# Second products of experts 2 to 4 in four forms: one bank, two banks by turns, columns in runs of 128 or of 32

## The chip, the core and the metric

The kernel runs on one core of a Trainium2 chip. The metric is the device time of one execution in microseconds, the median of the timed runs.

## The reference

Attention with band masks (2 batches, 8 heads, 576 positions, width 64) gives 1152 tokens of width 512. They go through a mixture of four experts, weighted by normalised domain probabilities, and then through one wider gated layer:

```python
def _moe_ref(x, domain_probs, w1, w2):
    p = domain_probs / (domain_probs.sum(-1, keepdims=True) + 1e-09)
    for e in range(E):
        h = np.maximum(x @ w1[e], 0.0)
        out += p[:, e:e + 1] * (h @ w2[e])
def _moe2_ref(x, w_in, w_out):
    h = x @ w_in
    g = h * (1.0 / (1.0 + np.exp(-1.702 * h)))
    return g @ w_out
```

The hidden width is 1024 in an expert and 2048 in the last layer. The weights of the last layer come as 64-bit floats.

## The kernel before

Every matrix is split into a high part of the type that TensorE multiplies in one pass (float32r, 4 bytes) and the low remainder, so each product of the algorithm is three matmuls: high by high, high by low, low by high.

The first expert is computed beside the attention (lines 517 and 545 to 547). From the second expert on the work goes in steps `s`. A step is 256 of the hidden columns: steps 4 to 15 are experts 2 to 4 (four steps each), steps 16 to 23 the last layer. Each step is done for two blocks of tokens, `c` = 0 with 512 tokens (four tiles of 128) and `c` = 1 with 640 (five tiles).

- `first2(s, c, slots)` makes the hidden values. Seven block products by a Strassen-like scheme, each six matmuls of 256 (`c` = 0) or 320 (`c` = 1) columns, are written to four tiles of the PSUM pool `ps`, named ga to gd in the trace (line 781). ACT, DVE and POOL combine them (lines 796 to 839) into `h`, high and low. The last of these steps is put on a list, `deferred`.
- `second2(s, c, slots)` (lines 849 to 879) multiplies `h` with the second weights. For each tile of tokens it takes one whole PSUM bank (128x512 floats) of the pool `pacc`, which has three, by turns: `pa0`, `pa1`, `pa2`. Six matmuls of 512 columns add up in it (lines 863 to 865, for two halves `o`). Then DVE multiplies by the expert's probability and adds to `acc` in SBUF (line 868, the eviction). After each tile one entry of `deferred` and one share of the queued side work (`slots`) are issued.

The side work is the preparation of coming weights: splitting (ACT line 685 and others, POOL lines 667 to 686), and the conversion of the 64-bit weights (ACT 727 and 728, DVE 733 and 737, POOL 738, stores and loads by SP). `due` says which lists are handed out during which call.

The order of the calls is written out by `order_of`: the first products of one block ahead of the second products of the block before. In the middle of experts 2 to 4 it reads: first products of (5, 1), second of (5, 0), first of (6, 0), second of (5, 1), and so on. Each engine executes its instructions in that order and waits on semaphores.

Of the kernel before, what the change touches and what calls it, by code (L numbers as in the profile page):

```python
# [8 lines left out]
F32 = mybir.dt.float32  # L9
# [3 lines left out]
AF = mybir.ActivationFunctionType  # L13
ALU = mybir.AluOpType
AX = mybir.AxisListType

P = 128
# [6 lines left out]
def fused_kernel(ctx: ExitStack, tc: tile.TileContext, q, k, v, dp, w1, w2, w_in, w_out, out):  # L24
# [17 lines left out]
    nc = tc.nc  # L42
    B, H, S, D = q.shape
    NT, DM = out.shape
    E, _, FF1 = w1.shape
# [17 lines left out]
    pacc = ctx.enter_context(tc.tile_pool(name="pacc", bufs=1, space=bass.MemoryType.PSUM))  # L63
# [8 lines left out]
    pw = const.tile([P, NC * NTI, E], F32, name="pw")  # L72
# [6 lines left out]
    acc = accp.tile([P, NC * NTI, DM], F32, name="acc")  # L79
# [417 lines left out]
    pa = {}  # L497
# [66 lines left out]
    SM, SE = NF * E, NF * E + F2 // 2  # L564
    TILES = (range(0, 4), range(4, 9))
    queue = []
    turn_ = [0]
# [6 lines left out]
    def slot(left):  # L574

        for _ in range(-(-len(queue) // max(left, 1))):
            queue.pop(0)()
# [186 lines left out]
    deferred = []  # L764
# [80 lines left out]
    def slots():  # L845
        slot(left[0])
        left[0] -= 1

    def second2(s, c, slots):
        n = N_[c]  # L850
        e, fp = divmod(s, NF)
        moe = e < E
        h = hbuf2.pop((s, c))
        wh, wl = wt[s, 1]
        for i, t in enumerate(TILES[c]):

            end = s == SE - 1 and c == 1 and i == len(TILES[c]) - 1
            for cols in (slice(0, DM // 2), slice(DM // 2, DM)) if end else (slice(0, DM),):
                pt = pacc.tile([P, 512], F32, tag=f"pa{turn_[0] % 3}", name=f"q{s}_{t}_{cols.start}")[:, cols]
                turn_[0] += 1  # L860
                for o in range(2):
                    hi, lo = (h[:, y, o * 2 * n + i * P:o * 2 * n + (i + 1) * P] for y in range(2))
                    nc.tensor.matmul(pt, hi, wh[:, o, cols], start=o == 0, stop=False)  # L863
                    nc.tensor.matmul(pt, hi, wl[:, o, cols], start=False, stop=False)  # L864
                    nc.tensor.matmul(pt, lo, wh[:, o, cols], start=False, stop=o == 1)  # L865
                dst = acc[:, t, cols]
                if moe:
                    nc.vector.scalar_tensor_tensor(dst, pt, pw[:, t, e:e + 1], dst, op0=ALU.mult, op1=ALU.add)  # L868
                elif s == SM and c == 1:
                    nc.vector.tensor_scalar_mul(dst, pt, 0.5)  # L870
                elif s == SM:
                    nc.scalar.activation(dst, pt, AF.Copy, scale=0.5)
                else:
                    nc.vector.scalar_tensor_tensor(dst, pt, 0.5, dst, op0=ALU.mult, op1=ALU.add)  # L874
                if s == SE - 1:
                    nc.sync.dma_start(out=out[t * P:(t + 1) * P, cols], in_=dst)
            if deferred:
                deferred.pop(0)()
            slots()

    seq = [("e", 0, c, f) for c in range(NC) for f in range(F1)]
    it_now = [0]
# [127 lines left out]
    for kind, (s, c) in pe:  # L1010
        todo = due(kind, s, c)
        if todo:
            assert not queue
            left[0] = todo[0]
            bg(*todo[1])
        (first2 if kind == "1" else second2)(s, c, slots)
# [29 lines left out]
```

## Time and profile before

| | |
|---|---|
| two timed runs | 649.69 and 650.69 us, median 650.19 |
| profiled execution, span from first to last instruction | 647.3 us |
| its own time beside the span | not recorded apart; the median is 2.9 us above the span |
| PE busy | 637.3 us, 98% |
| DVE, ACT, POOL busy | 419.6, 288.9, 356.2 us |
| matmuls | 4065, of which 362 stand on each of lines 863 to 865 |

PE is TensorE's matmuls, PEld its weight loads, which run beside them. Times of instructions are microseconds from the start of the span, unless marked ns. The duration of a matmul overlaps with that of the next, so what a product costs is read from start to start. [...]

### The profile page before, as it was taken

The numbers are of one execution on the slowest core, as the hardware profiler recorded it, in microseconds if no ns is written. First come the engines' busy times: TensorE is split into PE (matmuls) and PEld (weight loads), VectorE is DVE, ScalarE is ACT, GpSimd is POOL, SyncE is SP. The second block draws the span as 40 slices with busy tenths as digits, with TensorE's granted clock in tenths as the row PEclk, the third lists the DMA queues.
The fourth block names the chain that finished last, engine by engine and source line by source line (L and its number), as shares of the span: only waits on it lengthen the run. The fifth ranks groups of instructions, "written<-read, shape, count | busy, mean of one in ns | idle before, by whom it ended". The sixth has DMA issues, their size and how long they took to land.

```text
span 647.3 us, 10999 instructions
## 1 busy us (share of the span) xinstructions
PE 637.3 (98%) x4065; PEld 564.1 (87%) x4065; DVE 419.6 (65%) x882; ACT 288.9 (45%) x669; POOL 356.2 (55%) x362
## 2 busy tenths in 40 slices
PE   9999999999999999999999999999899999999998
PEld 6788888898898998998988988988798898898896
DVE  5775553296667667667667667557856767667655
ACT  6774342134444453443543544445745443444321
POOL 5433220367577587587578568586467744553300
PEclk9999999999999999999999999999999999999999
DMA  8966300004255345454445453211002111100003
GB/s 209 233 170 155 126 1 2 1 1 146 65 164 163 100 162 162 110 161 157 132 147 150 143 155 134 98 67 32 34 2 65 66 34 52 46 2 1 2 0 147
DMA packets 50149, 61.41 MB, mean 95 GB/s; under 512 B 20464, under 2 KB 32688, under 8 KB 50096
## 3 DMA queue, kind: packets, MB, share of 16 engines
q1 hardware_dynamic: 50096, 60.72, 31.1%
q8 instruction: 32, 0.52, 0.3%
q14 instruction: 21, 0.17, 0.1%
HBM read 49.96 MB, written 10.75 MB: 94 GB/s over the span
## 4 chain that ended last, share of the span: by engine, by line
PE 90%; DVE 4%; ACT 3%; issue 1%; POOL 1%; DVEq 0%; ACTq 0%
PE q L863 12%; PE q L865 12%; PE q L864 12%; PE gd L781 9%; PE ga L781 9%; PE gc L781 9%; PE g L517 8%; PE gb L781 4%; PE pa L545 3%; PE pa L547 3%; PE pa L546 3%; DVE cc L825 1%; PE spin L418 1%; DVE h L829 1%; ACT th L822 1%
## 5 line engine op out<-in xcount | busy, mean ns | idle before, releaser
L863 PE MATMUL q<-w2h,h 128*128 128x512 f32 (+1 forms) x362 | 143.4, 396 | 1.3 <-ACT xf L648 1.1
L865 PE MATMUL q<-w2h,h 128*128 128x512 f32 (+1 forms) x362 | 142.9, 395 | 0.0
L864 PE MATMUL q<-w2l,h 128*128 128x512 f32 (+1 forms) x362 | 142.9, 395 | 0.0
L868 DVE SCALAR_TENSOR_TENSOR acc<-q,pw,acc 128x512 f32<-128x512 f32 x108 | 80.5, 748 | 36.7 <-PE q L865 35.2
L738 POOL TENSOR_TENSOR m<-m,sd 128x512 int32<-128x512 int32 x32 | 41.9, 1308 | 78.3 <-issue 46.6
L863 PEld LDWEIGHTS q<-w2h,h 128*128 128x128 f32 x362 | 68.2, 188 | 17.2 <-ACT xf L648 1.5
L865 PEld LDWEIGHTS q<-w2h,h 128*128 128x128 f32 x362 | 68.1, 188 | 16.3
L864 PEld LDWEIGHTS q<-w2l,h 128*128 128x128 f32 x362 | 68.2, 188 | 14.7
L805 POOL TENSOR_TENSOR cc<-s,u 128x256 f32<-128x256 f32 (+1 forms) x40 | 37.4, 935 | 58.5 <-DVE s L803 56.2
L675 POOL TENSOR_TENSOR wsl<-ss,wsh 128x512 fp32r<-128x512 f32 x40 | 53.8, 1366 | 19.8 <-ACT wsh L674 19.8
L686 POOL TENSOR_TENSOR w2l<-st,w2h 128x512 fp32r<-128x512 f32 x40 | 51.9, 1301 | 5.0 <-ACT w2h L685 5.0
L874 DVE SCALAR_TENSOR_TENSOR acc<-q,acc 128x512 f32<-128x512 f32 (+1 forms) x64 | 42.7, 678 | 15.0 <-PE q L865 13.9
L671 POOL TENSOR_TENSOR wal<-st,wah 128x512 fp32r<-128x512 f32 (+1 forms) x40 | 50.2, 1271 | 2.5 <-ACT wah L670 2.5
L796 ACT ACTIVATE s<-ga 128x256 f32<-128x256 f32 (+1 forms) x40 | 16.4, 409 | 77.7 <-PE ga L781 77.7
L781 PE MATMUL ga<-xh,wah 128*128 128x256 f32 (+1 forms) x160 | 47.5, 297 | 0.0
L781 PE MATMUL ga<-xl,wah 128*128 128x256 f32 (+1 forms) x160 | 47.3, 296 | 0.0
L781 PE MATMUL ga<-xh,wal 128*128 128x256 f32 (+1 forms) x160 | 47.2, 295 | 0.0
L685 ACT ACTIVATE w2h<-st 128x512 fp32r<-128x512 f32 x40 | 25.0, 627 | 48.2 <-PE q L864 48.2
L801 DVE TENSOR_TENSOR u<-gb,s 128x256 f32<-128x256 f32 (+1 forms) x40 | 18.2, 456 | 39.4 <-PE gb L781 36.8
L781 PE MATMUL gd<-t,wah 128*128 128x256 f32 (+1 forms) x160 | 33.5, 298 | 1.7 <-DVE s L803 1.7
L815 ACT ACTIVATE h<-cc 128x768 fp32r<-128x768 f32 (+1 forms) x24 | 22.3, 928 | 27.6 <-POOL cc L805 23.9
L826 ACT ACTIVATE h<-cc 128x256 fp32r<-128x256 f32 (+3 forms) x32 | 22.0, 686 | 27.1 <-DVE cc L825 27.0
(458 smaller groups left out, 1632.0 us busy)
## 6 DMA issues: line engine op xcount, KB each, us to landing
st<-in_moe_w_dram SPq DMA_DIRECT2D x32, 512.0 KB, 5.4
sd<-in_moe_w_in_dram SPq DMA_DIRECT2D x16, 512.0 KB, 4.2
sd<-in_moe_w_out_dram SPq DMA_DIRECT2D x16, 512.0 KB, 4.1
w<-m SPq DMA_DIRECT2D x32, 256.0 KB, 4.4
st<-w SPq DMA_DIRECT2D x16, 512.0 KB, 3.3
out_dram<-acc SPq DMA_DIRECT2D x8, 256.0 KB, 2.0
v10big<-in_v_dram SPq DMA_DIRECT2D x2, 144.0 KB, 4.4
v11big<-in_v_dram SPq DMA_DIRECT2D x2, 144.0 KB, 2.8
```

The source lines that it names most:

```text
L517: nc.tensor.matmul(pt[:, :C], w[:, kt, fs], xx[:, kt, c * C:(c + 1) * C], start=first and y == 0, stop=not todo and y == len(products[x]) - 1)
L671: fns.append(lambda dst=dst, srcs=srcs: nc.gpsimd.tensor_tensor(out=al[:, dst], in0=srcs, in1=ah[:, dst].bitcast(F32), op=ALU.subtract))
L675: fns.append(lambda dst=dst: nc.gpsimd.tensor_tensor(out=sl[:, dst], in0=sums[:, dst], in1=sh[:, dst].bitcast(F32), op=ALU.subtract))
L686: fns.append(lambda o=o: nc.gpsimd.tensor_tensor(out=lo[:, o], in0=t[:, o], in1=hi[:, o].bitcast(F32), op=ALU.subtract))
L738: nc.gpsimd.tensor_tensor(out=m.bitcast(I32), in0=m.bitcast(I32), in1=t.bitcast(I32)[:, :, 0], op=ALU.add)
L781: nc.tensor.matmul(bank_[:, :n], wz[:, y, m, :], xz, start=start and m == 0 and z == 0, stop=m == 1 and z == 2, skip_group_check=not start)
L805: nc.gpsimd.tensor_tensor(out=cc[:, 3], in0=s75, in1=u2, op=ALU.add)
L863: nc.tensor.matmul(pt, hi, wh[:, o, cols], start=o == 0, stop=False)
L864: nc.tensor.matmul(pt, hi, wl[:, o, cols], start=False, stop=False)
L865: nc.tensor.matmul(pt, lo, wh[:, o, cols], start=False, stop=o == 1)
L868: nc.vector.scalar_tensor_tensor(dst, pt, pw[:, t, e:e + 1], dst, op0=ALU.mult, op1=ALU.add)
L874: nc.vector.scalar_tensor_tensor(dst, pt, 0.5, dst, op0=ALU.mult, op1=ALU.add)
```

## The change

In experts 2 to 4 the step number modulo 4 picks a form for the second products. Form 0 is as before. Form 1 takes the tiles in pairs: two banks are taken, and each of the six matmuls is issued for the one tile and then for the other; both evictions and two shares of side work follow the pair (a fifth tile stands alone). Forms 2 and 3 are as before, but a matmul reads its 512 weight columns and writes its bank in another order: the columns are cut into runs of 128 (form 2) or 32 (form 3), and all even runs come before all odd ones, on both sides alike.

```diff
-        for i, t in enumerate(TILES[c]):
+        form = s % 4 if moe else 0
+        tiles = list(enumerate(TILES[c]))
+        size = 2 if form == 1 else 1
+        for some in (tiles[x:x + size] for x in range(0, len(tiles), size)):
...
-                pt = pacc.tile([P, 512], F32, tag=f"pa{turn_[0] % 3}", name=f"q{s}_{t}_{cols.start}")[:, cols]
-                turn_[0] += 1
+                banks = []
+                for i, t in some:
+                    banks.append(pacc.tile([P, 512], F32, tag=f"pa{turn_[0] % 3}", name=f"q{s}_{t}_{cols.start}")[:, cols])
+                    turn_[0] += 1
                 for o in range(2):
-                    hi, lo = (h[:, y, o * 2 * n + i * P:o * 2 * n + (i + 1) * P] for y in range(2))
-                    nc.tensor.matmul(pt, hi, wh[:, o, cols], start=o == 0, stop=False)
-                    nc.tensor.matmul(pt, hi, wl[:, o, cols], start=False, stop=False)
-                    nc.tensor.matmul(pt, lo, wh[:, o, cols], start=False, stop=o == 1)
+                    for y in range(3):
+                        for (i, t), pt in zip(some, banks):
+                            hi, lo = (h[:, z, o * 2 * n + i * P:o * 2 * n + (i + 1) * P] for z in range(2))
+                            left_, right_ = ((hi, wh), (hi, wl), (lo, wh))[y]
+                            to, by = pt, right_[:, o, cols]
+                            if form >= 2:
+                                to, by = (z.rearrange("p (b a w) -> p a b w", a=2, w=128 if form == 2 else 32)
+                                          for z in (to, by))
+                            nc.tensor.matmul(to, left_, by, start=o == 0 and y == 0, stop=o == 1 and y == 2)
...
+            for _ in some:
+                if deferred:
+                    deferred.pop(0)()
+                slots()
```

On PE, in step 5 at the third and fourth tile of `c` = 0, before. A row is line, operation, bank's tile (q5_3 is step 5, tile 3) <- weights (w2h high, w2l low) and h, shape, and the semaphores waited for:

```order
L864 MATMUL q5_1_0_2530<-w2l_5_2188,h5_0_2369 128x512
L865 MATMUL q5_1_0_2530<-w2h_5_2187,h5_0_2369 128x512
L863 MATMUL q5_2_0_2540<-w2h_5_2187,h5_0_2369 128x512
L864 MATMUL q5_2_0_2540<-w2l_5_2188,h5_0_2369 128x512
L865 MATMUL q5_2_0_2540<-w2h_5_2187,h5_0_2369 128x512
L863 MATMUL q5_2_0_2540<-w2h_5_2187,h5_0_2369 128x512
L864 MATMUL q5_2_0_2540<-w2l_5_2188,h5_0_2369 128x512
L865 MATMUL q5_2_0_2540<-w2h_5_2187,h5_0_2369 128x512
L863 MATMUL q5_3_0_2549<-w2h_5_2187,h5_0_2369 128x512 [waits DVE_49]
```

The same place after:

```order
L875 MATMUL q5_0_0_2519<-w2l_5_2188,h5_0_2369 128x512 [waits Pool_49]
L875 MATMUL q5_1_0_2520<-w2l_5_2188,h5_0_2369 128x512
L875 MATMUL q5_0_0_2519<-w2h_5_2187,h5_0_2369 128x512
L875 MATMUL q5_1_0_2520<-w2h_5_2187,h5_0_2369 128x512
L875 MATMUL q5_2_0_2540<-w2h_5_2187,h5_0_2369 128x512
L875 MATMUL q5_3_0_2541<-w2h_5_2187,h5_0_2369 128x512 [waits DVE_49]
L875 MATMUL q5_2_0_2540<-w2l_5_2188,h5_0_2369 128x512
L875 MATMUL q5_3_0_2541<-w2l_5_2188,h5_0_2369 128x512
```

The wait of tile 3 for the eviction of tile 0, which had the same bank, stood twelve products behind tile 0's last product; now two products of other tiles stand between, the last one of tile 1 and the first one of tile 2.

On DVE at the same place, before (acc is an eviction, h the low part of the hidden values, m the word conversion):

```order
L839 TENSOR_TENSOR cc5_1_2449<-gd5_1_2444,u2_5_1_2447 128x320 [waits PE_49]
L868 SCALAR_TENSOR_TENSOR acc_92<-q5_0_0_2519,pw_87,acc_92 128x512 [waits PE_49]
L818 SCALAR_TENSOR_TENSOR h5_1_2498<-cc5_1_2449,h5_1_2498 128x960 [waits Activation_49]
L733 TENSOR_SCALAR m4_2528<-sd4_2327 128x512 [waits DMAHW5_49,DMAHW0_49]
L868 SCALAR_TENSOR_TENSOR acc_92<-q5_1_0_2530,pw_87,acc_92 128x512 [waits PE_49]
L737 SCALAR_TENSOR_TENSOR m4_2528<-sd4_2327,m4_2528 128x512 [waits DVE_49]
L868 SCALAR_TENSOR_TENSOR acc_92<-q5_2_0_2540,pw_87,acc_92 128x512 [waits PE_49]
```

And after:

```order
L839 TENSOR_TENSOR cc5_1_2449<-gd5_1_2444,u2_5_1_2447 128x320 [waits PE_49]
L879 SCALAR_TENSOR_TENSOR acc_92<-q5_0_0_2519,pw_87,acc_92 128x512 [waits PE_49]
L879 SCALAR_TENSOR_TENSOR acc_92<-q5_1_0_2520,pw_87,acc_92 128x512 [waits PE_49]
L818 SCALAR_TENSOR_TENSOR h5_1_2498<-cc5_1_2449,h5_1_2498 128x960 [waits Activation_49]
L733 TENSOR_SCALAR m4_2536<-sd4_2327 128x512 [waits DMAHW5_49,DMAHW0_49]
L737 SCALAR_TENSOR_TENSOR m4_2536<-sd4_2327,m4_2536 128x512 [waits DVE_49]
L879 SCALAR_TENSOR_TENSOR acc_92<-q5_2_0_2540,pw_87,acc_92 128x512 [waits PE_49]
```

The second eviction moved ahead of the low part of h and of the word conversion.

In step 7 (form 3) the first tile's six products read as follows after the change; the shape names the columns as 2 by 8 by 32, and the first product has a wait of PE for its own semaphore, which before it had not:

```order
L875 MATMUL q7_0_0_3023<-w2h_7_2691,h7_0_2873 128x2x8x32 [waits PE_49]
L875 MATMUL q7_0_0_3023<-w2l_7_2692,h7_0_2873 128x2x8x32 [waits Pool_49]
L875 MATMUL q7_0_0_3023<-w2h_7_2691,h7_0_2873 128x2x8x32 x2
L875 MATMUL q7_0_0_3023<-w2l_7_2692,h7_0_2873 128x2x8x32 [waits Pool_49]
L875 MATMUL q7_0_0_3023<-w2h_7_2691,h7_0_2873 128x2x8x32
```

The order of these products is as before. The awaited product is one of tile 6 of step 6, which had the same bank and is issued 55 products earlier.

## Rows read from the trace of the kernel before

**Rows 1.** The page: span, busy time of three engines, chain that ended last.

```profile
span 647.3 us, 10999 instructions
...
PE 637.3 (98%) x4065; PEld 564.1 (87%) x4065; DVE 419.6 (65%) x882; ACT 288.9 (45%) x669; POOL 356.2 (55%) x362
...
PE 90%; DVE 4%; ACT 3%; issue 1%; POOL 1%; DVEq 0%; ACTq 0%
```

**Rows 2.** Idle time of PE by releaser: us in total, times, longest us.

```profile
PE gd L781 <- DVE s L803: 1.7, 3, 0.9
...
PE q L863 <- ACT xf L648: 1.1, 1, 1.1
...
PE gc L781 <- POOL wsl L675: 0.2, 1, 0.2
```

**Rows 3.** Stretches: length, busy PE, PEld, DVE, ACT, POOL; granted clock, DMA share, GB/s.

```profile
177.00:201.00 24.00, 24.00 (x142) 21.54 (x141) 16.12 (x28) 10.56 (x20) 16.68 (x16) 1.00 0.49 143
391.00:415.00 24.00, 24.00 (x141) 21.54 (x140) 16.33 (x29) 10.72 (x20) 16.77 (x16) 1.00 0.33 121
```

**Rows 4.** PE in time, step 5: start us, us, instruction; 320-, 512-, 256-column products.

```profile
188.69 0.31 PE L781 MATMUL ga<-xh,wah 128*128 128x320 f32 x1
...
194.85 0.39 PE L863 MATMUL q<-w2h,h 128*128 128x512 f32 x1
195.08 0.39 PE L864 MATMUL q<-w2l,h 128*128 128x512 f32 x1
...
196.01 0.39 PE L865 MATMUL q<-w2h,h 128*128 128x512 f32 x1
196.24 0.40 PE L863 MATMUL q<-w2h,h 128*128 128x512 f32 x1
...
200.46 0.28 PE L781 MATMUL ga<-xh,wah 128*128 128x256 f32 x1
...
205.48 0.39 PE L863 MATMUL q<-w2h,h 128*128 128x512 f32 x1
...
212.50 0.31 PE L781 MATMUL ga<-xh,wah 128*128 128x320 f32 x1
```

**Rows 5.** The chain around 121 us: start us, us, what; 384-column products.

```profile
121.16 2.11 PE g L517 x12
```

**Rows 6.** The evictions of the second products: ns min/median/max, first and last start.

```profile
L868 DVE SCALAR_TENSOR_TENSOR acc<-q,pw,acc x108: 735/751/752, 172.6 to 448.3; 128x512 f32<-128x512 f32 x108
```

**Rows 7.** DVE in time beside the four tiles of step 5.

```profile
195.05 0.49 DVE L839 TENSOR_TENSOR cc<-gd,u 128x320 f32<-128x320 f32 x1 [0.39 <-PE gd L781]
...
196.44 0.75 DVE L868 SCALAR_TENSOR_TENSOR acc<-q,pw,acc 128x512 f32<-128x512 f32 x1 [0.90 <-PE q L865]
...
197.11 1.15 DVE L818 SCALAR_TENSOR_TENSOR h<-cc,h 128x960 fp32r<-128x960 f32 x1
```

**Rows 8.** PE behind a wait for DVE, near 425 us, in time.

```profile
424.92 0.47 DVE L803 TENSOR_TENSOR s<-gd,s 128x320 f32<-128x320 f32 x1
...
424.94 0.31 PE L781 MATMUL gc<-xh,wsl 128*128 128x320 f32 x1
...
425.45 0.30 PEld L781 LDWEIGHTS gd<-t,wah 128*128 128x128 f32 x2 [0.47 <-DVE s L803]
...
425.45 0.56 PE L781 MATMUL gd<-t,wah 128*128 128x320 f32 x2 [0.21 <-DVE s L803]
...
425.85 0.30 PE L781 MATMUL gd<-t,wal 128*128 128x320 f32 x1
```

**Rows 9.** PE in time: last product of gc, first of gb.

```profile
190.30 0.31 PE L781 MATMUL gc<-t,wsl 128*128 128x320 f32 x1
190.44 0.46 PE L781 MATMUL gb<-t,wsh 128*128 128x320 f32 x2
190.74 0.31 PE L781 MATMUL gb<-t,wsl 128*128 128x320 f32 x1
```

More of the change, by code (lines that the diff above doesn't have):

```diff
@@ L854, in second2 @@
         wh, wl = wt[s, 1]
-        for i, t in enumerate(TILES[c]):
-            end = s == SE - 1 and c == 1 and i == len(TILES[c]) - 1
+        form = s % 4 if moe else 0
+        tiles = list(enumerate(TILES[c]))
+        size = 2 if form == 1 else 1
+        for some in (tiles[x:x + size] for x in range(0, len(tiles), size)):
+            end = s == SE - 1 and c == 1 and some[0][0] == len(TILES[c]) - 1
             for cols in (slice(0, DM // 2), slice(DM // 2, DM)) if end else (slice(0, DM),):
-                pt = pacc.tile([P, 512], F32, tag=f"pa{turn_[0] % 3}", name=f"q{s}_{t}_{cols.start}")[:, cols]
-                turn_[0] += 1
+                banks = []
+                for i, t in some:
+                    banks.append(pacc.tile([P, 512], F32, tag=f"pa{turn_[0] % 3}", name=f"q{s}_{t}_{cols.start}")[:, cols])
+                    turn_[0] += 1
@@ L861, in second2 @@
                 for o in range(2):
-                    hi, lo = (h[:, y, o * 2 * n + i * P:o * 2 * n + (i + 1) * P] for y in range(2))
-                    nc.tensor.matmul(pt, hi, wh[:, o, cols], start=o == 0, stop=False)
-                    nc.tensor.matmul(pt, hi, wl[:, o, cols], start=False, stop=False)
-                    nc.tensor.matmul(pt, lo, wh[:, o, cols], start=False, stop=o == 1)
[L866 to L879, printed above, removed]
+                    for y in range(3):
[7 more added lines that the diff above has]
+                            nc.tensor.matmul(to, left_, by, start=o == 0 and y == 0, stop=o == 1 and y == 2)
@@ new lines, in second2 @@
+                for (i, t), pt in zip(some, banks):
+                    dst = acc[:, t, cols]
+                    if moe:
+                        nc.vector.scalar_tensor_tensor(dst, pt, pw[:, t, e:e + 1], dst, op0=ALU.mult, op1=ALU.add)
+                    elif s == SM and c == 1:
+                        nc.vector.tensor_scalar_mul(dst, pt, 0.5)
+                    elif s == SM:
+                        nc.scalar.activation(dst, pt, AF.Copy, scale=0.5)
+                    else:
+                        nc.vector.scalar_tensor_tensor(dst, pt, 0.5, dst, op0=ALU.mult, op1=ALU.add)
+                    if s == SE - 1:
+                        nc.sync.dma_start(out=out[t * P:(t + 1) * P, cols], in_=dst)
```

## The prediction

> **What bounds the kernel now.** I read the page first: PE is busy 98% of a 647.3 us span, and 90% of the chain that ended last is PE [rows 1]. Next the waits of PE: outside the attention stage there are three entries that matter, 3.0 us together, none in the second products of experts 2 to 4 [rows 2]. [...]
>
> A busy PE does not give the price of a product, since durations overlap (a 512-column product shows 0.39 us, the next one starts 0.23 us later). I therefore go by starts [rows 4]. From 194.85 to 200.46 us stand 24 products of 512 columns (4 tiles of 6): 5.61/24 = 233.8 ns each. From 205.48 to 212.50 stand 30: 234.0 ns. From 188.69 to 194.85 stand 42 products of 320 columns: 146.7 ns. From 200.46 to 205.48 stand 42 of 256: 119.5 ns. The line through the last two is 0.425 ns a column and 10.7 ns for each product. It gives 173.9 ns for 384 columns, and 2.11/12 = 175.8 ns was found [rows 5]; for 512 it gives 228.3, 5.5 ns less than found. These three numbers (0.425, 10.7 and 5.5 ns) are all that the trace has for the change's three disputed prices.
>
> **The change part by part.** Steps 4 to 15 are concerned, three for each form, each with 9 tiles of 6 products: 54 a step, 162 a form, 648 together; the 108 evictions [rows 6] are the same 12 times 9. The number of products, weight loads, evictions and DMAs stays as it is. Forms 0 (steps 4, 8, 12) and all steps from 16 on keep their order.
>
> *Form 1, two banks by turns: rate.* Does a product run faster when the one before it wrote another bank? Before, the sixth product of a tile starts at 196.01 and the first of the next tile, in another bank, at 196.24: 0.23 us, the spacing inside a tile too (194.85 to 195.08) [rows 4]. I take 0. The lower end is that alternation saves the whole 5.5 ns: 162 x 5.5 = -0.9 us; the upper end by the same row is 0.
>
> *Form 1: banks.* There are three banks, and a pair takes two. The second pair needs the free one and the one that the first pair's first tile has just filled. In the order after, the second tile of the second pair waits for DVE in its first product, right behind one product that may go. Worked out from a pair's start: the first tile's last product is the eleventh, at 10 x 0.234 = 2.34 us. Its eviction starts 0.43 us after that product's start (196.01 to 196.44) [rows 4, 7] and takes 0.75 us [rows 6], so it ends at 3.52. PE follows an end of DVE by 0.06 us (424.92 + 0.47 = 425.39 to 425.45), and the first two products after such a wait take 0.40 us where 2 x 0.147 is usual, 0.11 more, since the weight load had waited too [rows 8]. The product was due as the fourteenth, at 3.04 us. Wait: 3.52 + 0.06 - 3.04 = 0.54, with the restart 0.65 us. Behind it in PE's queue stand the rest of the pair and everything after, so it is lost whole. One such place per block of tiles: four tiles are two pairs, five are two pairs and a single, and the single's bank was emptied during the second pair. Two blocks in each of three steps: 6 x 0.65 = **3.9 us**. Lower end: no restart loss and no semaphore, 6 x 0.48 = 2.9 us. Upper end: DVE has just begun its longest instruction there, 1.15 us [rows 7], when the tile is done: 6 x 1.80 = 10.8 us. I take 3.9, because in the order after both evictions stand directly behind the cc instruction, which ends at 195.54, two microseconds before the tile is done [rows 7].
>
> *Form 1: what is moved on DVE, POOL and SP.* The low part of h (1.15 us) now stands behind two evictions, and starts about 2 us later; it ends near 200.2 us and is read by the next block of second products from 205.48 on [rows 4], 5 us of cover. The queued side work of one tile (word conversion, weight splitting, their stores and loads) moves by one tile, 1.4 us, behind the pair. It feeds the next step's weights; PE waited for POOL's weights 0.2 us in the whole run [rows 2]. I cost both at 0. If that cover were gone, a delay of 1.4 us in three steps would cost 4 us.
>
> *Forms 2 and 3: waits.* The order after has a new wait of PE for its own semaphore on 26 first products of a tile in and right behind these steps. It is for a product of the block before, so it is met long ago. The kernel before has such a wait on the first gb product of these steps, and there the spacing is as elsewhere (190.30, 190.44) [rows 9]: 0.
>
> *Forms 2 and 3: rate.* The 512 columns are read and written in 4 runs of 128 (form 2) or 16 runs of 32 (form 3), even runs first. Each run is unbroken on both sides, and the number of columns is the same. No product in the trace has a broken operand. Nearest rows: below, a column order that removes the 5.5 ns, 324 x 5.5 = -1.8 us. Above, each run priced as if it were a product of its own, 10.7 ns: form 2 has three starts more, 32 ns x 162 = 5.2 us; form 3 fifteen more, 160 ns x 162 = 26.0 us; together 31.2 us. And the far end: the whole stream at half rate, 324 x 217.6 ns = 70.5 us. I take 0, as the row of 384 columns is nearest: columns cost 0.425 ns, and only what is issued anew costs more.
>
> [...]
>
> **Sum.** Span 647.3 + 3.9 = 651.2 us. The two timed runs have a median of 650.19, 2.9 us more than the profiled span, for what lies around it: 651.2 + 2.9 = **654.1 us**, +0.6%. About 2%, 13 us, is what a measurement of this kernel can tell from no change.
>
> **The rivals.**
> 1. Slower, by a start-up for each run: the operand walk of PE stops at every jump for what a product's issue costs. 654.1 + 31.2 = 685.3 us. For it: products do have a fixed part, 10.7 ns. Against: that part also holds the change of weights, which a run doesn't need. It decides from 9.1 us on (13 less 3.9), which is 3.7 ns for each of form 3's extra runs. Chance 0.10. A quarter of that price (7.8 us) gives 661.9, still within 2%: 0.08.
> 2. Slower, by half rate in every broken product: 654.1 + 70.5 = 724.6 us. For it only that 512 columns already cost 5.5 ns more than the line, as if long writes met a limit. Chance 0.07.
> [...]
> 3. The reordering helps: the 5.5 ns go in all 486 changed products, -2.7 us, 651.4; at the very most each sinks to the bare columns (217.6 ns), -7.9 us, 646.2. Against: the switch of banks shows nothing in the trace. Chance 0.05.
> 4. The bank wait is long (DVE late, 10.8 us): 661.0 us. It is inside the forecast's own range and chance.
>
> **How the numbers follow.** The forecast has 0.70, with an own range of 651 to 661 (ends of the bank wait, less the 1.8 us that a better column order could give). Range 650 to 667: it takes in the forecast, the quarter price and half of rival 3, and leaves out rivals 1 and 2 at full price. Faster by over 2% (under 637.2) is out of reach even for rival 3: 0.01. Slower by over 2% is rivals 1 and 2: 0.17. Within 2%: 0.82.
>
> **What would show it.** Right: spacing of 234 ns in forms 1, 2 and 3 alike; six waits of PE for DVE of about 0.5 us in steps 5, 9 and 13, and no others new; the same granted clock. Wrong: a spacing above 290 ns in form 3 (rival 1 at a third of its price), above 400 ns in forms 2 and 3 (rival 2), under 230 ns in form 1 (rival 3), or no wait at the pairs, which would mean that the bank argument is false. The prediction fails if the broken products cost more than 28 ns each on the mean.

## The result, and the profile after

The kernel after takes 653.62 us, the median of two runs (653.30 and 653.94), beside 650.19 before. The ratio is 1.0051 with an interval of 1.0034 to 1.0069: half a per cent slower, which is no change by the 2% of this measurement, and the forecast of 654.1 us was right. The span grew by 4.2 us, from 647.3 to 651.5; the granted clock, a share of full speed, stayed at 1.00.

The page of the kernel after, in the same three places as [rows 1]:

```profile
span 651.5 us, 10997 instructions
...
PE 639.2 (98%) x4063; PEld 563.8 (87%) x4065; DVE 420.4 (65%) x882; ACT 289.4 (44%) x669; POOL 356.3 (55%) x362
...
PE 91%; DVE 3%; ACT 2%; issue 1%; POOL 1%; DVEq 0%; POOLq 0%; ACTq 0%
```

Nothing here tells where 4.2 us went: PE is still busy 98%, and the shares of the chain moved by a point. The waits of PE tell it (us in total, times, longest):

```profile
PE q L875 <- DVE acc L879: 2.2, 6, 0.4
PE gd L781 <- DVE s L803: 1.7, 3, 0.9
...
PE q L875 <- ACT xf L648: 1.1, 1, 1.1
...
PE gc L781 <- POOL wsl L675: 0.2, 1, 0.2
```

The lower three answer to [rows 2] and are the same to a tenth. The first is new: six waits of the second products for an eviction. Three stretches of the kernel after, with the columns of [rows 3]:

```profile
177.00:201.00 24.00, 23.63 (x138) 20.86 (x136) 15.02 (x26) 10.57 (x20) 15.90 (x15) 1.00 0.48 143
225.00:249.00 24.00, 24.00 (x140) 21.51 (x139) 16.30 (x29) 10.58 (x20) 16.59 (x15) 1.00 0.46 143
391.00:415.00 24.00, 23.26 (x135) 20.29 (x134) 16.80 (x28) 10.70 (x20) 16.56 (x15) 1.00 0.37 130
```

The first has the wait of one block of step 5 in it, and PE is idle for 0.37 us; the last has the waits of both blocks of step 13, and PE is idle for 0.74. In the middle one, with the second block of step 6 and nearly all of the first block of step 7 (forms 2 and 3), PE is never idle.

Now the second products in time. The first rows are four tiles of step 5 (form 1, with DVE beside PE); then the first product of four tiles of step 6 (form 2) and of step 7 (form 3), each with the first product behind its 24:

```profile
194.98 0.62 PE L875 MATMUL q<-w2h,h 128*128 128x512 f32 x2
...
197.31 0.87 PE L875 MATMUL q<-w2h,h 128*128 128x512 f32 x3
197.75 1.41 DVE L879 SCALAR_TENSOR_TENSOR acc<-q,pw,acc 128x512 f32<-128x512 f32 x2 [2.07 <-PE q L875]
198.55 0.19 PEld L875 LDWEIGHTS q<-w2h,h 128*128 128x128 f32 x1 [0.81 <-DVE acc L879]
198.55 0.50 PE L875 MATMUL q<-w2h,h 128*128 128x512 f32 x1 [0.37 <-DVE acc L879]
...
198.89 0.63 PE L875 MATMUL q<-w2l,h 128*128 128x512 f32 x2
199.07 1.15 DVE L818 SCALAR_TENSOR_TENSOR h<-cc,h 128x960 fp32r<-128x960 f32 x1
...
201.23 0.28 PE L781 MATMUL ga<-xh,wah 128*128 128x256 f32 x1
...
220.09 0.39 PE L875 MATMUL q<-w2h,h 128*128 128x512 f32 x1
...
225.70 0.28 PE L781 MATMUL ga<-xh,wah 128*128 128x256 f32 x1
...
243.91 0.40 PE L875 MATMUL q<-w2h,h 128*128 128x512 f32 x1
...
249.56 0.28 PE L781 MATMUL ga<-xh,wah 128*128 128x256 f32 x1
```

The row at 197.31 holds the products eleven to thirteen, so the thirteenth starts at 197.31 + 2 x 0.234 = 197.78. The fourteenth starts at 198.55, 0.77 us later, and the fifteenth 0.34 behind it. Where 2 x 0.234 = 0.47 is usual, 1.11 us went by: 0.64 us are lost. All six blocks look so: 0.766 to 0.773 and 0.334 to 0.339, 3.83 us together. The "idle" of 0.37 in the row is smaller, because it counts from the modelled end of the product before; the loss is read from the starts. DVE takes the first tile from 197.75 on, so the eviction begins, as forecast, 0.43 to 0.44 us after the eleventh product's start.

Form 2 needs (225.70 - 220.09)/24 = 233.8 ns a product, as before [rows 4]; form 3 (249.56 - 243.91)/24 = 235.4, and 235.1 over all its blocks. That is 1.3 ns x 162 = 0.21 us. With 0.13 us by which the second products start later (171.16 instead of 171.03, ahead of anything that was changed) the sum is 3.83 + 0.21 + 0.13 = 4.2 us.

The evictions, against [rows 6], are as long as they were; their last start is 4.2 us later:

```profile
L879 DVE SCALAR_TENSOR_TENSOR acc<-q,pw,acc x108: 734/749/754, 172.8 to 452.5; 128x512 f32<-128x512 f32 x108
```

### The profile page after: what moved, and what is told of

Read it like the earlier page. It is cut to its first block, busy times and chain, and to the rows that moved or that the text cites. A ratio compares the mean times of both kernels' runs of the same rounds, so it can differ in the third digit from the quotient of the medians.

```text
span 651.5 us, 10997 instructions
## 1 busy us (share of the span) xinstructions
PE 639.2 (98%) x4063; PEld 563.8 (87%) x4065; DVE 420.4 (65%) x882; ACT 289.4 (44%) x669; POOL 356.3 (55%) x362
## 4 chain that ended last, share of the span: by engine, by line
PE 91%; DVE 3%; ACT 2%; issue 1%; POOL 1%; DVEq 0%; POOLq 0%; ACTq 0%
PE q L875 38%; PE gd L781 9%; PE ga L781 9%; PE gc L781 9%; PE g L517 8%; PE gb L781 5%; PE pa L545 3%; PE pa L547 3%; PE pa L546 3%; PE spin L418 1%; DVE acc L879 1%; DVE cc L825 0%; PE x L644 0%; POOL w2l L686 0%; DVE x L598 0%
## 5 line engine op out<-in xcount | busy, mean ns | idle before, releaser
L875 PE MATMUL q<-w2h,h 128*128 128x512 f32 (+1 forms) x724 | 231.8, 397 | 3.5 <-DVE acc L879 2.2
L875 PE MATMUL q<-w2l,h 128*128 128x512 f32 (+1 forms) x362 | 139.1, 395 | 0.0
L675 POOL TENSOR_TENSOR wsl<-ss,wsh 128x512 fp32r<-128x512 f32 x40 | 56.0, 1420 | 19.8 <-ACT wsh L674 19.8
L671 POOL TENSOR_TENSOR wal<-st,wah 128x512 fp32r<-128x512 f32 (+1 forms) x40 | 48.0, 1219 | 2.5 <-ACT wah L670 2.5
L829 DVE TENSOR_TENSOR h<-cc,h 128x256 fp32r<-128x256 f32 (+3 forms) x32 | 28.7, 898 | 8.2 <-ACT h L826 6.4
L517 PE MATMUL g<-xh,wh 128*128 128x384 f32 x96 | 33.0, 344 | 0.6 <-ACT xh L327 0.6
```

The costliest lines, as they stand in the source:

```text
L517: nc.tensor.matmul(pt[:, :C], w[:, kt, fs], xx[:, kt, c * C:(c + 1) * C], start=first and y == 0, stop=not todo and y == len(products[x]) - 1)
L671: fns.append(lambda dst=dst, srcs=srcs: nc.gpsimd.tensor_tensor(out=al[:, dst], in0=srcs, in1=ah[:, dst].bitcast(F32), op=ALU.subtract))
L675: fns.append(lambda dst=dst: nc.gpsimd.tensor_tensor(out=sl[:, dst], in0=sums[:, dst], in1=sh[:, dst].bitcast(F32), op=ALU.subtract))
L829: nc.vector.tensor_tensor(out=hl[:, sub], in0=cc[:, sub], in1=hh[:, sub].bitcast(F32), op=ALU.subtract)
L875: nc.tensor.matmul(to, left_, by, start=o == 0 and y == 0, stop=o == 1 and y == 2)
```

## The experiments

All have the kernel after as their base. Experiments e5, e6 and e10 were timed in one run each; the others were timed several times beside the kernel before, whose median lay between 649.6 and 650.1 us in these series.

**Form 1 alone, and forms 2 and 3 alone.** First the two halves of the change apart.

```diff
-        form = s % 4 if moe else 0
+        form = 1 if moe and s % 4 == 1 else 0
```

> Form 1 alone (steps 5, 9, 13 in pairs; all other steps one bank a tile, columns in order). Theory (the wait for a bank at each second pair is the whole cost): six waits, each with a spacing of 0.77 us in place of 0.234 and a restart of 0.34, 0.64 us lost each, 3.8 us over the kernel before, about 654.0. Rival (the broken column orders cost a part of the 3.4 us): clearly less than 3.4 us over, 652 or below.

```diff
-        form = s % 4 if moe else 0
+        form = s % 4 if moe and s % 4 != 1 else 0
```

> Forms 2 and 3 alone (steps 5, 9, 13 as before). Theory: form 2 at 234 ns a product as before, form 3 about 1.2 ns above, 162 x 1.2 = 0.2 us: 650.4, no change that can be measured. Rival (broken orders cost): 1.5 us or more over the kernel before, with spacings of 239 ns or more in both forms.

Form 1 alone took 654.02 us, ratio 1.006 (1.0045 to 1.0075). Forms 2 and 3 alone took 650.64, ratio 1.0004 (0.9994 to 1.0014). The waits of form 1 alone have the same entry as after, to a tenth:

```profile
PE q L875 <- DVE acc L879: 2.3, 6, 0.4
```

So the cost is in the pairs, but for the 0.2 us of form 3. In the other half form 2 showed 233.7 to 234.2 ns and form 3 234.7 to 235.1.

**The bank wait, longer and shorter.** If it is the full bank that costs, the price must follow the place of the one product that needs it. In e3 the tile with the full bank is issued first in a second pair; in e8 three products of the other tile go ahead of it. In both, form 1 stands alone.

```diff
...
-                        for (i, t), pt in zip(some, banks):
+                        for (i, t), pt in list(zip(some, banks))[::-1 if len(some) == 2 and some[0][0] else 1]:
```

> Form 1 alone, and in each second pair the tile whose bank is still full goes first. Theory (bank wait): its first product is now due one product earlier, 0.234 us, and comes at the same end of the eviction, so each of six waits is 0.23 us longer, 0.88 us lost each: 5.2 us over the kernel before, about 655.4. Rival (the pairs cost through the change of banks or through DVE's moved work, wherever the full bank stands): the same 3.8 us as form 1 alone.

```diff
...
-                for o in range(2):
-                    for y in range(3):
-                        for (i, t), pt in zip(some, banks):
+                todo = [(o, y, it_, pt) for o in range(2) for y in range(3) for it_, pt in zip(some, banks)]
+                if len(some) == 2 and some[0][0]:
+                    mine = [[z for z in todo if z[2][0] == it_[0]] for it_ in some]
+                    todo = mine[0][:3] + [z for both in zip(mine[1][:3], mine[0][3:]) for z in both] + mine[1][3:]
+                for o, y, (i, t), pt in todo:
...
```

> Form 1 alone, and in each second pair the tile with the free bank makes its first three products before the other tile begins. Theory (bank wait): the full bank's first product is due at 15 x 0.234 = 3.51 us from the pair's start, and its bank is free at about 3.58: a wait of under 0.1 us, with the restart 0.1 to 0.2 us each, 0.4 to 1.1 us in all, 650.6 to 651.3. Rival (pairs cost by themselves): 3 to 4 us over the kernel before.

Full bank first: 655.36 us, ratio 1.0080 (1.0065 to 1.0095). Full bank late: 651.32 us, ratio 1.0030 (1.0008 to 1.0052); nine of its ten runs lie between 650.4 and 651.8 us, and one took 657.8, which nothing here explains. PE's waits of e3, and the place that answers to 197.31 above:

```profile
PE q L875 <- DVE acc L879: 3.6, 6, 0.6
```

```profile
197.90 0.64 PE L875 MATMUL q<-w2h,h 128*128 128x512 f32 x2
...
199.14 0.72 PE L875 MATMUL q<-w2h,h 128*128 128x512 f32 x2 [0.61 <-DVE acc L879]
```

The last product ahead starts at 197.90 + 0.23 = 198.13 and the waiting one at 199.14: 1.01 us, 0.24 more than above, which is the one product that no longer stands between. The same place in e8:

```profile
198.50 1.04 PE L879 MATMUL q<-w2h,h 128*128 128x512 f32 x3
199.38 0.63 PE L879 MATMUL q<-w2l,h 128*128 128x512 f32 x2
```

From 198.50 to 199.38 are three spacings, 0.88 us where 0.70 is usual. In the six blocks the waiting product starts 0.296 to 0.303 us behind the one ahead and the next 0.334 to 0.343 behind it: 0.17 us is lost in each block, most of it in the restart (0.34 - 0.23 = 0.11). The price goes as the distance in products between the end of the tile that holds the bank and the first product that wants it.

**Many more pairs.** In e9 every step of experts 2 to 4 has form 1, so 24 blocks instead of six.

```diff
-        form = s % 4 if moe else 0
+        form = 1 if moe else 0
```

> Form 1 in all twelve steps: the suspected cost four times over. Theory: 24 second pairs at 0.64 us are 15.3 us, and where three blocks of second products follow each other near the end of expert 4 a pair follows a pair once or twice more: 16 to 17 us over the kernel before, 666 to 667. Rival (part of the wait is taken up again elsewhere, as PE's slack grows): under 12 us.

It took 665.92 us, ratio 1.0252 (1.0235 to 1.0269). The waits:

```profile
PE q L875 <- DVE acc L879: 8.9, 24, 0.4
```

Each of the 24 has 0.767 to 0.774 and 0.333 to 0.340 again: 24 x 0.64 = 15.4 us, and 665.92 is 16.3 above the 649.6 of the kernel before in this series. Most of the other 0.9 us stands in the waits list too: the entry of line 803 has 2.2 us instead of 1.7, and one of 0.3 us for ACT's line 796 is new. The waits don't help each other or eat slack elsewhere; the cost of the pairs is linear.

**Pairs without a full bank.** In e4 each block has one pair, its second and third tile; three banks are enough, since a single tile stands on either side.

```diff
-        form = s % 4 if moe else 0
+        form = 1 if moe else 0
-        size = 2 if form == 1 else 1
-        for some in (tiles[x:x + size] for x in range(0, len(tiles), size)):
+        cuts = (0, 1, 3, *range(4, len(tiles) + 1)) if form == 1 else range(len(tiles) + 1)
+        for some in (tiles[x:y] for x, y in zip(cuts, cuts[1:])):
```

> All twelve steps: one tile alone, then one pair by turns, then the rest alone. Theory (only a bank that is still full costs): a tile alone after the pair takes a bank that was emptied while the pair ran, and a pair finds two empty banks, so there is no wait: within 0.5 us of the kernel before. Rival (turning between two banks costs in itself, 3.8 us for the 12 pairs of form 1, 0.32 us a pair): 24 pairs, 7.6 us over, about 658.

This missed: 652.69 us, ratio 1.0048 (1.0033 to 1.0063), though the mechanism held. All 21 blocks up to 415 us are without a wait, at 233.8 and 234.2 ns a product. Nearly three microseconds are lost at the end of expert 4, where the waits list has two entries that before did not have:

```profile
PE q L875 <- DVE acc L879: 1.1, 1, 1.1
...
PE ga L781 <- ACT s L796: 0.7, 1, 0.7
```

And DVE and PE in time at the longer of the two:

```profile
443.12 0.75 DVE L879 SCALAR_TENSOR_TENSOR acc<-q,pw,acc 128x512 f32<-128x512 f32 x1
443.78 1.03 DVE L587 TENSOR_TENSOR t<-xt,t 128x512 fp32r<-128x512 f32 x1
444.74 1.40 DVE L879 SCALAR_TENSOR_TENSOR acc<-q,pw,acc 128x512 f32<-128x512 f32 x2
445.54 0.50 PE L875 MATMUL q<-w2h,h 128*128 128x512 f32 x1 [1.11 <-DVE acc L879]
```

Here the side work that a pair hands out together is preparation for the last layer (line 587). It stood on DVE ahead of the pair's evictions for 1.03 us, and PE wanted their bank. The other wait, 0.7 us for ACT near 424 us, comes where side work on POOL runs 1.6 us later than before (line 667 first at 418.51 instead of 416.92) and ACT waits 1.99 us for it instead of 0.84; that the pairs moved it fits, but no run takes it apart. So alternating two banks is free by itself, and side work moved by one tile is not free everywhere: in steps 5, 9 and 13 it is, at the end of expert 4 it cost.

**How broken may a product be?** Forms 2 and 3 cost almost nothing. Shorter runs, on both sides and without pairs, show where that ends: runs of 16, 8, 4 and 2 columns by step.

```diff
-        size = 2 if form == 1 else 1
+        size = 1
-                            if form >= 2:
+                            if moe:
-                                ... w=128 if form == 2 else 32)
+                                ... w=(16, 8, 4, 2)[form])
```

> No pairs; all twelve steps in broken order, runs of 16 columns in steps 4, 8, 12, of 8 in 5, 9, 13, of 4 in 6, 10, 14 and of 2 in 7, 11, 15. [...] Theory B (each run has a small price, 1.2 ns for the 12 further runs of 32 in place of 128, 0.1 ns a run): 237, 240, 247 and 260 ns, about 5 us in all. Theory C (short runs fall to half rate somewhere below 32): 450 ns from that width on, 35 us for each width concerned.

First product of four tiles, and the first one behind the 24, in runs of 16, 8, 4 and 2:

```profile
172.19 0.41 PE L875 MATMUL q<-w2h,h 128*128 128x512 f32 x1
...
177.95 0.28 PE L781 MATMUL ga<-xh,wah 128*128 128x256 f32 x1
...
196.34 0.39 PE L875 MATMUL q<-w2h,h 128*128 128x512 f32 x1
...
201.86 0.28 PE L781 MATMUL ga<-xh,wah 128*128 128x256 f32 x1
...
219.96 0.39 PE L875 MATMUL q<-w2h,h 128*128 128x512 f32 x1
...
225.53 0.27 PE L781 MATMUL ga<-xh,wah 128*128 128x256 f32 x1
...
243.66 0.62 PE L875 MATMUL q<-w2h,h 128*128 128x512 f32 x1
...
254.52 0.30 PE L781 MATMUL ga<-xh,wah 128*128 128x256 f32 x1
```

The differences over 24 are 240.0, 230.0, 232.1 and 452.5 ns. A product with 128 runs of 4 was as quick as a straight one, 232.1 ns beside 233.8; with 256 runs of 2 it took 452.5, nearly twice as long. The whole kernel took 686.2 us in one run. A price for each run's start would have grown from step to step; none shows. Why runs of 16 take 6 ns more and runs of 8 take 4 ns less than straight, this experiment does not tell.

**On which side?** In e6 one side alone has the broken order, the other stays straight, in runs of 2 (read, then write) and of 4 (read, then write).

```diff
...
-                                to, by = (z.rearrange("p (b a w) -> p a b w", a=2, w=128 if form == 2 else 32)
-                                          for z in (to, by))
+                                order = [z.rearrange("p (b a w) -> p a b w", a=2, w=2 + form // 2 * 2) for z in (to, by)]
+                                plain_ = [z.rearrange("p (a b w) -> p a b w", a=2, w=2 + form // 2 * 2) for z in (to, by)]
+                                to, by = (plain_[0], order[1]) if form % 2 == 0 else (order[0], plain_[1])
```

> No pairs; broken order on one side alone: steps 4, 8, 12 read the weights in runs of 2 and write the bank straight, 5, 9, 13 read straight and write in runs of 2, 6, 10, 14 read in runs of 4, 7, 11, 15 write in runs of 4. The columns of these products land in other places than the reference's, so the result is that of another computation with the same work. If short runs are free on both sides: 234 to 237 ns in all four. If a price belongs to the reading of SBUF, it shows in the first and third group alone; if to the writing of PSUM, in the second and fourth alone.

The two cases with runs of 2: 30 products that read so, then 24 that write so.

```profile
187.96 0.61 PE L876 MATMUL q<-w2h,h 128*128 128x512 f32 x1
...
201.54 0.32 PE L781 MATMUL ga<-xh,wah 128*128 128x320 f32 x1
...
207.71 0.39 PE L876 MATMUL q<-w2h,h 128*128 128x512 f32 x1
...
213.32 0.28 PE L781 MATMUL ga<-xh,wah 128*128 128x256 f32 x1
```

Reading in runs of 2 takes 13.58/30 = 452.7 ns, writing in runs of 2 takes 5.61/24 = 233.8. In runs of 4 reading takes 231.7 and writing 234.2. So the doubling is wholly on the side that reads the weights in SBUF, and a product that writes its bank in pieces of 8 bytes took 233.8 ns, as a straight one does.

**The order of reading.** Runs of 8 and 4 had been quicker than straight, runs of 16 slower. In e10 the second products of steps 4 to 15 and 18 to 21, and the first products of most of these steps, have orders from a table: `(a, w)` takes runs of `w` columns, each `a*w` columns behind the one before, in `a` passes, on the reading and the writing side alike.

```diff
+SECOND = {4: (2, 8), 5: (4, 8), 6: (8, 8), 7: (16, 8), 8: (32, 8), 9: (2, 4), 10: (4, 4), 11: (8, 4), 12: (16, 4), ...
...
-                            if form >= 2:
+                            if s in SECOND:
+                                a_, w_ = SECOND[s]
+                                to, by = (z.rearrange("p (b a w) -> p a b w", a=a_, w=w_) for z in (to, by))
```

> A map of column orders, no pairs: every step has one order for its second products and, in 13 of them, one for its first products (256 and 320 columns). An order is a pair (a, w): runs of w columns, each a-th run in a row, the rest in further rounds, so the jump between runs is a x w columns. Second products (2, 8), (4, 8), (8, 8), (16, 8), (32, 8), (2, 4), (4, 4), (8, 4), (16, 4), (32, 4), (64, 4), (2, 64) in steps 4 to 15, (4, 16), (8, 16), (4, 32), (4, 64) in steps 18 to 21. Theory A (only the length of a run decides): 230 ns for all runs of 8, 232 for all of 4, 240 for 16, 235 for 32 and 234 for 64, whatever the jump. Theory B (the jump decides, as the reading of one column line meets the reading of another): runs of 4 and 8 differ among themselves by 3 ns or more with a. For the first products: under both theories runs of 8 and 4 change them as the second ones, by 1 to 2%, 117 to 118 and 144 to 145 ns in place of 119.5 and 146.7.

From start to start, in ns, straight last:

| products | quickest | slowest | some others | straight |
|---|---|---|---|---|
| second, 512 | (4,4) 226.6 | (16,4) 278.0, (32,4) 266.9 | (2,8) 230.6, (16,8) 230.2, (2,4) 231.8, (8,16) 231.8, (4,8) 233.0, (4,16) 237.9, (8,8) 243.1, (8,4) 245.8, (64,4) 246.8 | 233.8 |
| first, 256 | (4,8) 113.5 | (16,4) 134.9 | (4,4) 116.1, (2,4) 117.8, (8,8) 120.1 | 119.5 |
| first, 320 | (4,4) 141.3 | (16,4) 166.7 | (4,8) 146.1, (2,4) 146.8, (8,8) 155.0, (8,4) 159.4 | 146.7 |

The trace of e10 at the two ends of the first line, (4,4) and then (16,4), 24 products each:

```profile
317.30 0.39 PE L883 MATMUL q<-w2h,h 128*128 128x512 f32 x1
...
322.74 0.28 PE L789 MATMUL ga<-xh,wah 128*128 128x256 f32 x1
...
365.52 0.44 PE L883 MATMUL q<-w2h,h 128*128 128x512 f32 x1
...
372.18 0.29 PE L789 MATMUL ga<-xh,wah 128*128 128x256 f32 x1
```

That is 226.7 and 277.5 ns, with the same runs of 16 bytes. The length of a run does not decide, then; where the next run lies does, but not by the jump alone: (16,8) and (32,4) both jump 128 columns and stand at 230.2 and 266.9. Nor does an order always have one price: (8,8) took 245.8 ns a product in one block of step 6 (from 219.76 us) and 241.0 in the other (from 230.60), and (8,16) 233.9 and 230.1. The kernel took 657.89 us in one run.

**The quickest orders everywhere.** e12 gives all second products, the last layer's too, the order (4,4); e11 gives the first products (4,8) and (4,4) as well.

```diff
-        size = 2 if form == 1 else 1
+        size = 1
-                            if form >= 2:
+                            if True:
+                                a_, w_ = (4, 4)
+                                to, by = (z.rearrange("p (b a w) -> p a b w", a=a_, w=w_) for z in (to, by))
```

> Only the second products of steps 4 to 23, in runs of 4, each fourth run in a row. Theory: 1074 x 7.3 = 7.8 us less than the kernel before, about 642. Rival (scatter by place): 3 us or less below the kernel before, with steps on both sides of 234 ns.

```diff
+                    to, by = bank_[:, :n], xz
...
+                        a_, w_ = (4, 8) if c == 0 else (4, 4)
+                        to, by = (u.rearrange("p (b a w) -> p a b w", a=a_, w=w_) for u in (to, by))
...
```

> The orders that were fastest in the map, in all steps 4 to 23: second products in runs of 4, each fourth run in a row (226.6 ns against 233.9), first products of 256 columns in runs of 8, each fourth (113.5 against 119.5), of 320 in runs of 4, each fourth (141.3 against 146.7). Theory (the order sets the spacing, wherever the tiles lie): 1074 x 7.3 = 7.8 us, 840 x 6.0 = 5.0 us, 840 x 5.4 = 4.5 us, 17 us less than the kernel before, about 632.5. Rival (in the map each order had one step, and the gain hung on where that step's tiles lay): the spacings scatter between steps and the total is 5 us or less below the kernel before.

e12 took 642.60 us, ratio 0.9891 (0.9874 to 0.9907), with 225.8 to 227.3 ns in every block but those between 430 and 502 us, where PE has waits in the kernel before too. That is 1.1% faster, clear of one but under the 2% of a change. e11 took 635.89, ratio 0.9784 (0.9770 to 0.9799): 14.2 us and 2.2% faster than the kernel before, from nothing but the order in which columns are read and written. Its page and its waits:

```profile
span 634.0 us, 10997 instructions
...
PE 622.2 (98%) x4063; PEld 554.7 (87%) x4065; DVE 419.1 (66%) x882; ACT 291.2 (46%) x669; POOL 355.3 (56%) x362
```

```profile
PE gd L785 <- DVE s L807: 2.5, 3, 1.1
...
PE q L879 <- DVE acc L885: 0.5, 1, 0.5
PE q L879 <- DVE acc L889: 0.4, 1, 0.4
```

PE has 15 us less to do. It came 3.4 us short of the 632.5 expected. Nearly half is in these rows: the first has 0.8 us more than [rows 2], and the other two are longer than before: the products at 483.2 and 496.0 us start 0.87 and 0.80 us behind the one ahead, their counterparts before 0.38 and 0.54, 0.8 us more together. Another 1.3 us is in the spacings: where PE has no wait, the second products of e11 take 227.1 to 227.9 ns instead of 226.6, and those of 256 columns 114.0 instead of 113.5. The rest was not traced.

## Why the prediction was right, step by step

- *What bounds the stage.* PE alone, busy for all 24.00 us of both stretches of [rows 3], so that each wait comes out whole. Six waits of 0.64 us are 3.8 of the 4.2 us by which the span grew, and 24 of them (e9) are 15.4 of 16.3 us: shown.
- *The bank wait, 0.65 us each.* 0.64 was found in all six: a wait of 0.53 to 0.54 and a restart of 0.10 to 0.11, where the sum had 0.54 and 0.11. The step that carried it was the count of products between the tile's end and the product that waits; e3 (0.24 more) and e8 (0.47 less) move it by one and two products of 0.234, and e4 takes it away. The upper end, DVE busy with its longest instruction at that moment, did not occur: the low part of h stood behind both evictions (199.07), as read from the order. The restart is read from the 0.34 behind each wait, less 0.23.
- *The rate of alternating banks, 0.* In the pairs without a wait (e4) the spacing is 233.8 and 234.2 ns. Shown.
- *Forms 2 and 3, 0.* Form 2 nothing, form 3 1.3 ns a product, 0.2 us in all. Rival 1, a price for each run, needed 3.7 ns for each extra run in form 3; found was 1.3/15 = 0.09 ns, and e5 shows no steady growth up to 128 runs. It falls.
- *Half rate, rival 2.* It does not come at runs of 32 (235.1 ns), but it exists: runs of 2 on the reading side took 452.7 ns (e6). Written in runs of two fp32 values, a product stayed at 233.8 ns there.
- *Rival 3, the reordering helps.* It was judged on the wrong ground (the switch of banks, which says nothing of column orders). For the orders of this change it falls, but other orders do gain, up to 7 ns a second product: more than the 5.5 ns that the prediction counted on, less than the 16 ns that it gave as the most. That forms 2 and 3 lay so near to straight was partly luck, since e10 has orders that take 33 to 44 ns more, by a cause that stays open.
- *Moved side work, 0.* Right in steps 5, 9 and 13. As a general statement it is wrong, as e4's 1.1 us behind line 587 shows.
- *Waits of PE for itself, 0.* None appears in the waits, and the spacing behind them is the usual one: step 7's first product, which has one, starts 0.14 us behind a product of 320 columns (243.77, 243.91) and 0.24 ahead of the next.
- *The 2.9 us beside the span.* All runs on record that list both, the kernel before among them, have 1.7 to 1.9 us between time and span (after: 653.30 and 651.5). By that the profile before is of an execution of about 649.1 us, and about 1.1 of the 2.9 us is scatter between executions. The sum comes to the same as the median before plus 3.9 us; that it met the result to 0.5 us, inside that scatter, is luck.

## What to carry to other kernels

Where one engine is the bound, count instructions between the last use of a buffer and the first instruction that wants it again: alternating two tiles over three banks shortens that distance from twelve products to two, and the price follows in steps of one product. Read prices from start to start, since the idle time listed for PE understated its wait here (0.37 us where 0.64 was lost). And the order in which a matmul reads its columns is a free choice that was worth 2.2% here: try a few orders, on both sides alike, before taking the straight one for the best.

## What the runs showed of the hardware

A float32r product of 512 columns is one record of the trace, 233.8 ns from start to start in straight order; bf16 products of that shape stood 215 ns apart (before, line 418, from 4.45 us).

The spacing of a float32r product of 512 columns went from 226.6 to 278.0 ns with the order in which it takes its columns, read and written alike in runs of 16 bytes; straight reading, at 233.8, was not the quickest. The same held at 256 and 320 columns (113.5, there in runs of 32 bytes, to 134.9; 141.3 to 166.7). On which side this arises was separated for (2,2) and (2,4) alone (e6), not for these orders, and the slow orders stood in one step each. Runs of 8 bytes on the reading side took nearly double the time (452.7), on the writing side they were free (233.8).

Runs of 16 bytes, with all even ones ahead of all odd ones, took no longer than straight: 232.1 ns on both sides (e5), 231.7 on the reading side alone (e6).

Why (4,4) is quicker than straight and (16,4) slower stays open. That (4,4) is nearly the same in every step in e12 (225.8 to 227.3 ns, but for the blocks between 430 and 502 us) speaks against the place of one tile as its cause, while (8,8), with 245.8 and 241.0 ns in the two blocks of one step, shows that more than the order has a part; whether the weight loads, which run beside the products (PEld busy 21.54 of 24.00 us in [rows 3]), have a part in it was not tried.
